# Three and a half score tiles for images two to four, with column sums and small operations moved to other steps

## The chip, the cores and the metric

The kernel runs on one core of a Trainium2 chip. Its metric is the device time of one execution in microseconds (us); the figure to beat is the median of the runs shown. A core has a matrix engine (TensorE, PE in the rows; PEld is its loading of weights), a vector engine (VectorE, DVE), a scalar engine (ScalarE, ACT), GpSimd (POOL), and SyncE (SP), which here only issues transfers. Matrix products land in PSUM, which has eight banks for each of 128 partitions; everything else works in SBUF.

## What is computed

An attention over 4 images of 448 rows with 12 heads of 64, in which the heads are mixed before and after the softmax, and on its result (1,792 rows of 768) an RMS norm and a gated network:

```python
scores = scale * np.matmul(q, k.transpose(0, 1, 3, 2))
scores = np.einsum('bhij,hg->bgij', scores, w_pre)
scores = scores - np.max(scores, axis=-1, keepdims=True)
attn = np.exp(scores)
attn = attn / (np.sum(attn, axis=-1, keepdims=True) + 1e-09)
attn = np.einsum('bhij,hg->bgij', attn, w_post)
y = np.matmul(attn, v)                      # x: (4*448, 768), heads side by side
rms = np.sqrt(np.mean(x * x, axis=-1, keepdims=True) + 1e-06)
xn = x / rms * rms_g
g = xn @ w_gate
silu = g * (1.0 / (1.0 + np.exp(-g)))
out = silu * (xn @ w_val) @ w_out
```

## The kernel before

**Chunks and steps.** Each image's 448 rows are cut into four chunks (`n` counts them, 0 to 15, four to an image) of 120, 120, 110 and 98 rows. A chunk is worked off in 6, 6, 6 and 5 *steps* `(n, p)`. This gives 92 steps, numbered 0 to 91 here. The first steps of the chunks are 0, 6, 12, 18 | 23, 29, 35, 41 | 46, 52, 58, 64 | 69, 75, 81, 87. The attention runs from 0 to about 345 us; then comes the gated network.

**What stands in a step.** `part_a` emits every engine's work by hand, step by step, and each engine takes its own in that order. In step t, which works on `(n, p)`:
- PE makes the *premix* `sp`, the scores of 20 query rows mixed over the heads. It is four products of 64x64 weights `wk_pre` with `r`, two for each half of the rows of PE, into two PSUM banks.
- DVE takes the two row maxima `nm` (`rowmax`). ACT makes the two exponentials `e` (`expo`) and sums each as it goes. `norm` adds 1e-9 (`t`, DVE), takes the reciprocal (`rp`, DVE) and scales the weights of the second mix with it (`wn`, two operations on GpSimd).
- PE makes the *postmix* `pm` of the step before, which needs that step's `e` and `wn`. ACT and DVE copy a half each into `at_all` (`evac_a`).
- PE makes one or two pieces of `av`, attention times `v`, for an earlier pair of chunks (`av_at`). ACT copies finished ones into `xt` (`av_copy`).
- PE makes one *score unit* `qk` of a later chunk (`qk_at`): the products of `q` and `k` for a pair of heads, again four products into two banks. Its second half stands between the two halves of the premix, its first behind them. ACT copies one bank out into `st`, DVE the other (`qk_evac`). Transfers on SP's queue then regroup the rows of `st` into `r`, in which heads and rows lie as the premix wants them. `r` has three tiles, one for every third chunk.

**Units and their order.** A chunk has six score units, one a step, in a plain list: five ahead of step 0, then one for each of the steps 0 to 84. Steps 85 to 91 have none. A fourth chunk has only 98 rows but takes six units as well.

**Work on the side.** GpSimd squares and adds up finished rows (`sum_ops`: L318, L325, L332, L333), one operation a step up to step 80 and two from then on, emitted ahead of `norm`'s `wn`. When an image is complete, PE makes its column sums `pss` (`column_sums`, L347, into a bank of the score units); a chain of small operations turns them into the reciprocal root (`rsqrt`; DVE first, then GpSimd), and `x_scale_ops` follows. PE makes `pss` at the end of the steps 40, 63 and 84. From step 23 on DVE also converts the weights of the gated network, an operation of about 0.35 us a step (`first_w`, tile `wac`), and other small chains. `lows` are low halves of a split, emitted by `flush`. Loads of `q`, `k` and `v` are jobs with a fixed step (`job`).

Of the kernel before, what the change touches and what calls it, by code (L numbers as in the profile page):

```python
# [7 lines left out]
F32 = mybir.dt.float32  # L8
# [16 lines left out]
GROUPS = [12, 12, 12, 9]  # L25
# [26 lines left out]
def attention_moe(ctx: ExitStack, tc, q, k, v, wpre, wpost, mask, ident, wgv, wo, rms_g, out):  # L52
# [33 lines left out]
    wk_pre = cst.tile([128, 64], F32, name="wk_pre")  # L86
    wk = cst.tile([128, HR], F32, name="wk")

    msk = pro.tile([128, 2, RH], F32, name="msk", tag="ksm1")
    we = pro.tile([128, H], F32, name="we", tag="ksm2")  # L90
    wp = pro.tile([128, H], F32, name="wp", tag="ksm3")

    def load_consts():
        nc.sync.dma_start(msk.rearrange("p a r -> p (a r)"), mask)
        nc.sync.dma_start(we, wpre)
        nc.sync.dma_start(wp, wpost)

# [28 lines left out]
    held = []  # L126
# [7 lines left out]
    def qk_mm(n, hp):  # L134
# [6 lines left out]

        return [[lambda j=j, u=u: one(j, u) for u in range(2)] for j in range(2)]
# [8 lines left out]

    def qk_evac(n, hp, j):
        h, np_ = 2 * hp + j, PAIRS[n % NC]
        ps = qps[n, hp][j]
        if n == 0 and h < 1 or n == 1 and h < 2 * AHEAD:
            st = pro.tile([128, S], F32, name="st", tag="st", bufs=11)
        else:
            st = pq.tile([128, S], F32, name="st", tag="st", bufs=12)
        if j:
            nc.vector.tensor_copy(st, ps[:, :S])  # L160
        else:
            nc.scalar.activation(st, ps[:, :S], AF.Copy)
        for i, (lo, hi) in enumerate(((0, EARLY), (EARLY, 2 * np_)) if n == 0 else ((0, GROUPS[n % NC]),)):
            w, at_ = RH * (hi - lo), 2 * RH * lo
            if h < H - 1:
                parts = [(h, 2 * RH, at_, 2 * w)]
            else:
                parts = [(h, RH, at_, w), (64, RH, at_ + w, w)]
            for row, k_, src, many in parts:
                dst = rt[n][row : row + (k_ - 1) * GAP + 1 : GAP, lo:hi]  # L170
                if i:
                    held.append((dst, st[src : src + many]))
                else:
# [1086 lines left out]
```

## Time and profile before

| | us |
|---|---|
| median of 3 runs | 827.72 |
| lowest, highest | 825.3, 830.05 |
| profiled execution, own time | 822.48 |
| its span | 820.6 |
| PE busy | 794.4 |
| DVE busy | 634.5 |
| ACT busy | 507.3 |
| GpSimd busy | 350.4 |

The span goes from the first to the last recorded instruction; the execution's own time is a little longer. An engine's busy time counts the time in which at least one of its instructions runs. PE is near its limit on the average, but the average covers the gated network, where it hardly pauses, and the attention, where several engines take turns.

### The profile page before, as it was taken

What the parts mean: (1) busy time and instruction counts of PE and PEld (TensorE: products, weight loads), DVE (VectorE), ACT (ScalarE), POOL (GpSimd) and SP (SyncE); (2) the same over time, 40 slices, a digit from 0 to 9 for tenths busy, and PEclk for the clock granted to TensorE, in tenths of its full rate; (3) what the DMA queues carried; (4) which work ended last, traced back from release to release, by engine and by line L of the source; (5) the groups of instructions that cost most, each with busy time, mean ns of one, the idle gap of its engine ahead of it and who ended that gap; (6) DMA issues with size and microseconds to landing.
All of it is one profiled execution on the core that took longest, in us unless ns stands there. A gap on an engine that the chain in (4) does not pass through costs nothing.

```text
span 820.6 us, 26914 instructions
## 1 busy us (share of the span) xinstructions
PE 794.4 (97%) x10806; PEld 485.2 (59%) x10806; DVE 634.5 (77%) x1322; ACT 507.3 (62%) x1133; POOL 350.4 (43%) x467
## 2 busy tenths in 40 slices
PE   7899999999999989899999999999999999999998
PEld 2567777767776767655555555555555555555555
DVE  5777878888798867888788978997889676547562
ACT  3677778777776867664344454545444546969850
POOL 7212343454355435843624433426144359452310
PEclk9999999999999999999999999999999999999999
DMA  7777777777876754564255644754546446566641
GB/s 216 208 216 217 219 229 222 228 219 232 222 234 200 211 147 150 158 230 118 66 177 150 183 129 127 216 149 121 174 145 201 133 127 184 157 199 176 184 135 67
DMA packets 81902, 145.15 MB, mean 177 GB/s; under 512 B 10527, under 2 KB 72797, under 8 KB 81779
## 3 DMA queue, kind: packets, MB, share of 16 engines
q1 hardware_dynamic: 79982, 139.83, 57.0%
q0 software_dynamic: 832, 2.06, 1.0%
q8 instruction: 85, 1.39, 0.7%
q10 hardware_dynamic: 965, 1.56, 0.6%
q14 instruction: 38, 0.31, 0.1%
HBM read 72.83 MB, written 31.88 MB: 128 GB/s over the span
## 4 chain that ended last, share of the span: by engine, by line
PE 86%; DMA 8%; DVE 2%; issue 1%; ACT 1%; POOL 1%; SPq 0%; ACTq 0%; DVEq 0%; POOLq 0%
PE qk L140 7%; PE pm L226 7%; PE sp L187 7%; PE av L294 6%; PE pg L750 6%; PE pg L752 6%; PE pv L752 6%; PE pg L751 6%; PE pv L751 6%; PE pv L750 6%; DMA r<-st 6%; PE po L751 6%; PE po L750 6%; PE po L752 6%; DMA wraw<-in_wgv 1%
## 5 line engine op out<-in xcount | busy, mean ns | idle before, releaser
L187 PE MATMUL sp<-r,wk_pre 64*64 64x448 f32 x720 | 167.4, 542 | 5.4 <-DMA r<-st 3.5
L203 ACT ACTIVATE e<-sp,nm 128x448 f32<-128x448 f32 x180 | 114.3, 637 | 84.8 <-DVE nm L196 82.4
L140 PE MATMUL qk<-k,q 64*64 64x448 f32 x768 | 152.6, 559 | 5.9 <-DMA q<-in_q 4.1
L196 DVE TENSOR_REDUCE nm<-sp 128x1 f32<-128x448 f32 x180 | 110.3, 620 | 44.1 <-PE sp L187 27.4
L215 POOL TENSOR_SCALAR wn<-wk,rp 128x60 f32<-128x60 f32 x180 | 59.5, 345 | 181.8 <-DVE rp L212 109.7
L226 PEld LDWEIGHTS pm<-wn,e 60*64 60x64 f32 x5040 | 106.1, 134 | 37.6 <-POOL wn L215 23.8
L226 PE MATMUL pm<-wn,e 60*64 60x60 f32 x5040 | 106.7, 220 | 4.2 <-issue 4.1
L798 POOL TENSOR_TENSOR sg<-sg,u 128x448 f32<-128x448 f32 x36 | 45.9, 1275 | 151.2 <-ACT sg L795 106.7
L294 PE MATMUL av<-at_all,v 64*64 64x240 f32 (+6 forms) x1728 | 93.6, 316 | 4.6 <-issue 2.6
L750 PE MATMUL pv<-x,wh 128*128 128x448 f16 x264 | 93.0, 352 | 0.0
L752 PE MATMUL pv<-x,wl 128*128 128x448 f16 x264 | 93.0, 352 | 0.0
L752 PE MATMUL pg<-x,wl 128*128 128x448 f16 x264 | 93.0, 352 | 0.0
L751 PE MATMUL pv<-x,wh 128*128 128x448 f16 x264 | 93.0, 352 | 0.0
L751 PE MATMUL pg<-x,wh 128*128 128x448 f16 x264 | 93.0, 352 | 0.0
L750 PE MATMUL pg<-x,wh 128*128 128x448 f16 x264 | 93.0, 352 | 0.0
L750 PE MATMUL po<-h,fac 128*128 128x448 f16 (+1 forms) x258 | 89.8, 348 | 0.0
L751 PE MATMUL po<-h,fac 128*128 128x448 f16 (+1 forms) x258 | 89.8, 348 | 0.0
L752 PE MATMUL po<-h,fac 128*128 128x448 f16 (+1 forms) x258 | 89.8, 348 | 0.0
L750 PEld LDWEIGHTS <-wh 128*128 128x128 f16 x528 | 51.7, 98 | 48.2 <-issue 0.2
L751 PEld LDWEIGHTS <-wh 128*128 128x128 f16 x528 | 51.7, 98 | 48.3 <-issue 0.3
L752 PEld LDWEIGHTS <-wl 128*128 128x128 f16 x528 | 51.7, 98 | 48.2
L187 PEld LDWEIGHTS sp<-r,wk_pre 64*64 64x64 f32 x720 | 60.3, 133 | 27.2 <-ACT e L203 13.2
(167 smaller groups left out, 1567.3 us busy)
## 6 DMA issues: line engine op xcount, KB each, us to landing
r<-st SPq DMA_DIRECT2D x117, 210.0 KB
hraw<-td SPq DMA_DIRECT2D x84, 224.0 KB
wraw<-in_wgv SPq DMA_DIRECT2D x20, 768.0 KB
td<-keep SPq DMA_DIRECT2D x48, 224.0 KB
wraw<-in_wo SPq DMA_DIRECT2D x12, 768.0 KB
r<-st SPq DMA_DIRECT2D x44, 157.5 KB
v<-in_v SPq DMA_DIRECT2D x24, 256.0 KB
k<-in_k SPq DMA_DIRECT2D x24, 224.0 KB
```

What stands on the lines that cost most here:

```text
L140: nc.tensor.matmul(ps[j][m, :S], qt[n][sl, hp, m], kt[n // NC, hp][sl], start=True, stop=True)
L187: nc.tensor.matmul(o, wk_pre[sl], rt[n][sl, 2 * p + v_], start=True, stop=True)
L196: nc.vector.tensor_reduce(t, ps[:, :S], AX.X, ALU.max, negate=True)
L203: nc.scalar.activation(e, ps[:, :S], AF.Exp, bias=nmx.pop((n, p, u)), accum_out=sm[n, p][:, u : u + 1])
L215: nc.gpsimd.tensor_scalar(wn[n, p][:, u], wk, r[:, u : u + 1], 1.0, ALU.mult, ALU.mult)
L226: nc.tensor.matmul(o[:, :, at_], e_[sl, j : j + JT], w_[sl].rearrange("p (s i) -> p s i", s=2), start=True, stop=True)
L294: nc.tensor.matmul(x, vt[b, hp][sl, j, c_], a, start=(c_ == 0), stop=(c_ == JC - 1))
L750: nc.tensor.matmul(ps, a, xh[:, kk, at_], start=(kk == 0), stop=False)
L751: nc.tensor.matmul(ps, a, xl_[:, kk, at_], start=False, stop=False)
L752: nc.tensor.matmul(ps, a2, xh[:, kk, at_], start=False, stop=(kk == KT - 1))
L798: nc.gpsimd.tensor_tensor(h, sg, u, ALU.mult)
```

## The change

- **Shared score units.** In images two to four (chunks from 4 on) the chunks 0 to 2 of an image fill all 128 rows of a score tile: 8 more rows belong to the fourth chunk. What remains of the fourth chunk are 50 rows, which fit half a tile (64). A unit of such a *shared* chunk (`shared(n)`; n = 7, 11, 15) therefore makes four heads at once (`two`) instead of two, each bank holding two heads, and both row halves of PE write into one bank, bank by bank. Such a chunk takes three units instead of six.
- **`rest`.** The extra rows don't go into `r` but into a tile of their own, `rest`, to every second row of it (`rest_out`). The first and the last premix of a shared chunk read `rest` with a second variant of the weights `wk_pre`. GpSimd clears `rest` in the steps 3 and 7.
- **Order of the units.** A unit of chunk n stands no earlier than one step after the first of chunk n - 2. Together with the fewer units this leaves the steps 34, 35, 57, 58 and 80 to 91 without score products.
- **Column sums.** `pss` moves from the steps 40, 63 and 84 to 57, 79 and 84. Its chain keeps its bits in SBUF rather than in the PSUM bank, with three operations on DVE rather than four; `x_scale_ops` go one a step.
- **`t`** is made by GpSimd for all chunks but the last.
- Of the `lows` one is emitted behind the row maxima and up to two later in the step; loads of `q` and `k` get steps to suit; `st` becomes one tile with a place for each head; `first_w_ops(0)` starts six steps later.

```diff
+def shared(n):
+    return n >= NC and n % NC == NC - 1
...
-    wk_pre = cst.tile([128, 64], F32, name="wk_pre")
+    wk_pre = cst.tile([128, 2, 64], F32, name="wk_pre")
+    rest = cst.tile([128, 4, S], F32, name="rest")
...
         b, c = divmod(n, NC)
+        wide = 64 if shared(n) else 128
         if not hp:
-            qt[n] = pq.tile([128, H // 2, 128], F32, name=f"q{n}", tag="q", bufs=2)
-        hp = slice(hp, hp + many)
-        eng.dma_start(qt[n][:, hp], q[b, :, c, hp])
+            qt[n] = pq.tile([128, H // 2, wide], F32, name=f"q{n}", tag="q", bufs=2)
+        src = q[b, :, c * H // 2 * 128 + hp * wide : c * H // 2 * 128 + (hp + many) * wide]
+        eng.dma_start(qt[n][:, hp : hp + many].rearrange("p h w -> p (h w)"), src)
...
-    held = []
+    held, waiting = [], []
+    st_all = pq.tile([128, H, S], F32, name="st", tag="st")
...
+        def two(j, i):
+            sl, u = slice(64 * j, 64 * j + 64), (i + j) % 2
+            nc.tensor.matmul(ps[i][64 * u : 64 * u + 64, :S], qt[n][sl, 2 * hp + i], kt[n // NC, 2 * hp + i][sl], start=True, stop=True)
+
+        if shared(n):
+            return [[lambda j=j, i=i: two(j, i) for j in (i, 1 - i)] for i in range(2)]
         return [[lambda j=j, u=u: one(j, u) for u in range(2)] for j in range(2)]
...
+    def rest_out(n, half, st):
+        if shared(n):
+            for i in range(2):
+                for u in range(2):
+                    rows = slice(100 + 12 * u, 112 + 12 * u)
+                    nc.sync.dma_start(rest[rows, slot(n - 3 + i)], st[64 * u + 60 + 2 * i : 64 * u + 62 + 2 * i, :6])
+        else:
+            nc.sync.dma_start(rest[4 + half : 4 + half + 95 : 2, slot(n)], st[120:, 6 * half : 6 * half + 6])
...
+        last = shared(n)
+        kind = int(last and p in (0, PAIRS[-1] - 1))
...
+        def rows(sl, i):
+            if not kind:
+                return rt[n][sl, i - 2 * last]
+            return rest[sl, slot(n - 3 + (i if p == 0 else 2))]
 
...
             sl = slice(64 * u, 64 * u + 64)
-            nc.tensor.matmul(o, wk_pre[sl], rt[n][sl, 2 * p + v_], start=True, stop=True)
+            nc.tensor.matmul(o, wk_pre[sl, kind], rows(sl, 2 * p + v_), start=True, stop=True)
...
-        nc.vector.tensor_scalar(t, s, 1e-9, None, ALU.add)
+        (nc.gpsimd if n < NCHUNK - 1 else nc.vector).tensor_scalar(t, s, 1e-9, None, ALU.add)
...
-            sq[b, "ops"] = rsqrt(ps[:JP, :JC], b, const, nc.gpsimd, ps[:JP, JC : 2 * JC])
+            sq[b, "ops"] = rsqrt(ps[:JP, :JC], b, const, nc.gpsimd)
...
-        ops = [lambda o=o: nc.vector.tensor_scalar(o, v, 1.0 / DM, 1e-6, ALU.mult, ALU.add) for o in {id(x): x for x in (bits, var)}.values()]
-        ops += [
-            lambda: nc.vector.tensor_scalar(i, bits.bitcast(I32), 1, None, ALU.logical_shift_right),
+        ops = [
+            lambda: nc.vector.tensor_scalar(var, v, 1.0 / DM, 1e-6, ALU.mult, ALU.add),
+            lambda: nc.vector.tensor_scalar(i, var.bitcast(I32), 1, None, ALU.logical_shift_right),
...
-    for i, a in enumerate([(n, hp) for n in range(1, NCHUNK) for hp in range(H // 2)][AHEAD:]):
-        qk_at[i].append(a)
+    starts, t_ = {}, -1
+    for n in range(1, NCHUNK):
+        for hp in range(H // 4 if shared(n) else H // 2):
+            if n == 1 and hp < AHEAD:
+                continue
+            t_ = max(t_ + 1, first[n - 2] + 1 if n > 1 else 0)
+            starts.setdefault(n, t_)
+            qk_at[t_].append((n, hp))
...
-                job(6 * n - 16 + 3 * i, load_q, n, 3 * i, 3, nc.sync)
+                job(starts[n] - 5 + (1 if shared(n) else 3) * i, load_q, n, 3 * i, 3, nc.sync)
...
-    chain(first[4] + 29, lambda: first_w_ops(0), 2)
+    chain(first[4] + 35, lambda: first_w_ops(0), 2)
     chain(first[4] + 56, lambda: first_w_ops(1), 3)
...
-        t = first[NC * b + NC + 2] + (5 if b < B - 2 else 3)
-        for i in range(17):
-            last_at[t + max(i - 2, 0) // 3].append((sq_all, b, i))
-        chain(t, lambda b=b: x_scale_ops(b), 2 if b < B - 2 else 4)
+        t = (first[10] - 1, first[13] + 4, first[14] + 3)[b]
+        for i in range(16):
+            last_at[t + (max(i - 1, 0) if i < 4 else 3 + (i - 4) // 3)].append((sq_all, b, i))
+        chain((first[6] + 8, first[10] + 6, first[14] + 3)[b], lambda b=b: x_scale_ops(b), 1 if b < B - 2 else 4)
...
                 rowmax(*back(0))
-                flush()
+                flush(1)
                 expo(*back(0))
...
+            flush()
...
+            if t in (3, 7):
+                nc.gpsimd.memset(rest[:, t // 2 - 1 : t // 2 + 1], 0.0)
...
-    nc = bacc.Bacc("TRN2", target_bir_lowering=False, num_devices=1)
+    nc = bacc.Bacc("TRN2", target_bir_lowering=False, num_devices=1, dynamic_dma_scratch_size=8192)
```

On PE, from step 31 of the kernel before; `q_2195` are the queries of chunk 7, `r_123` and `r_121` the tiles of chunks 5 and 6, the rows from a first `sp` to the next `pm` are a step's premix and score unit (rows of the steps 32 and 33, which read likewise with `k_1` and `k_2`, stand between the first and the second piece):

```order
L187 MATMUL sp<-r_123,wk_pre 64x448 x2
L140 MATMUL qk<-k_0_827,q_2195 64x448 x2
L187 MATMUL sp<-r_123,wk_pre 64x448 x2
L140 MATMUL qk<-k_0_827,q_2195 64x448 x2
L226 MATMUL pm<-wn,e 64x2x30 x28
```

```order
L187 MATMUL sp<-r_123,wk_pre 64x448 x2
L140 MATMUL qk<-k_3_1036,q_2195 64x448 x2
L187 MATMUL sp<-r_123,wk_pre 64x448 x2
L140 MATMUL qk<-k_3_1036,q_2195 64x448 x2
L226 MATMUL pm<-wn,e 64x2x30 x28
L294 MATMUL av<-at_all,v_2_1337 64x220 x8
L187 MATMUL sp<-r_121,wk_pre 64x448 x2
L140 MATMUL qk<-k_4_1104,q_2195 64x448 x2
```

The second piece is step 34 and the start of 35, each with a unit of chunk 7. On PE in the changed kernel, from step 33 (`q_2131` are the queries of chunk 7, `r_126` and `r_124` the tiles of chunks 5 and 6):

```order
L232 MATMUL sp<-r_126,wk_pre 64x448 x2
L153 MATMUL qk<-k_5_1133,q_2131 64x448 x2
L232 MATMUL sp<-r_126,wk_pre 64x448 x2
L153 MATMUL qk<-k_4_1064,q_2131 64x448 x2
L271 MATMUL pm<-wn,e 64x2x30 x28
L339 MATMUL av<-at_all,v_1_1131 64x220 x4
L339 MATMUL av<-at_all,v_1_1131 64x2x55 x4
L232 MATMUL sp<-r_126,wk_pre 64x448 x4
L271 MATMUL pm<-wn,e 64x2x30 x28
L339 MATMUL av<-at_all,v_2_1291 64x220 x8
L232 MATMUL sp<-r_124,wk_pre 64x448 x4
```

Step 33 has the last unit of chunk 7, of four heads (two tiles of `k`); 34 and 35 go from the premix to the postmix with no unit between. Around the column sums, on PE before, the end of step 40 and the start of 41 (`k_4_3002`, `q_2672`: a unit of chunk 8; `sum_1495`: the sums of the first image):

```order
L294 MATMUL av<-at_all,v_5_2512 64x240 x4
L294 MATMUL av<-at_all,v_5_2512 64x2x60 x4
L347 MATMUL pss<-ones,sum_1495 112x1 x4
L187 MATMUL sp<-r_122,wk_pre 64x448 x2
L140 MATMUL qk<-k_4_3002,q_2672 64x448 x2
L187 MATMUL sp<-r_122,wk_pre 64x448 x2
```

and in the changed kernel, step 57 and the start of 58 (`sum_1446`: the same sums):

```order
L232 MATMUL sp<-r_124,wk_pre 64x448 x4
L271 MATMUL pm<-wn,e 64x2x30 x28
L339 MATMUL av<-at_all,v_2_2913 64x220 x8
L392 MATMUL pss<-ones,sum_1446 112x1 x4
L232 MATMUL sp<-r_125,wk_pre 64x448 x4
L271 MATMUL pm<-wn,e 64x2x30 x28
```

Before, a premix with a score unit stands behind `pss`; now a premix and a postmix. On DVE an ordinary step before reads

```order
L196 TENSOR_REDUCE nm<-sp 128x1 x2
L160 COPY st<-qk 128x448
L263 COPY at_all<-pm 128x2x42x5
L210 TENSOR_SCALAR t<-s 128x2
L212 RECIPROCAL rp<-t 128x2
L564 TENSOR_SCALAR wac<-wraw 128x384
```

and in the changed kernel

```order
L241 TENSOR_REDUCE nm<-sp 128x1 x2
L194 COPY st<-qk 128x448
L308 COPY at_all<-pm 128x2x42x5
L257 RECIPROCAL rp<-t 128x2
L613 TENSOR_SCALAR wac<-wraw 128x384
```

with `t` gone from between the copy and `rp`. On GpSimd two steps with additions of sums read so in the changed kernel (L363 is L318 of before, L370 is L325):

```order
L363 TENSOR_TENSOR xt_1692<-xt_1692,xt_1693 128x480
L255 TENSOR_SCALAR t<-s 128x2
L260 TENSOR_SCALAR wn<-wk,rp 128x60 x2
L370 TENSOR_TENSOR xt_1693<-xt_1692 128x480
L255 TENSOR_SCALAR t<-s 128x1
```

Here `t` stands behind the addition of its step and ahead of `wn`; before, `wn` alone stood there.

## Rows read from the trace of the kernel before

**Rows 1.** The page: the head.

```profile
span 820.6 us, 26914 instructions
```

**Rows 2.** Busy time by stretch: us, PE, PEld, DVE, ACT, POOL, PEclk, DMA, GB/s.

```profile
61.90:294.60 232.70, 222.75 (x5956) 172.97 (x5952) 192.13 (x517) 173.78 (x474) 100.88 (x220) 1.00 0.76 220
345.00:820.60 475.60, 472.40 (x2624) 247.24 (x2622) 360.70 (x618) 263.20 (x484) 194.32 (x145) 1.00 0.51 156
```

**Rows 3.** DVE's timeline, steps 30 and 31: start, us, what, [idle before <-releaser].

```profile
120.83 0.62 DVE L196 TENSOR_REDUCE nm<-sp 128x1 f32<-128x448 f32 x1
...
122.79 0.59 DVE L263 COPY at_all<-pm 128x420 f32<-128x420 f32 x1
123.29 0.16 DVE L210 TENSOR_SCALAR t<-s 128x2 f32<-128x2 f32 x1
123.55 0.17 DVE L212 RECIPROCAL rp<-t 128x2 f32<-128x2 f32 x1
...
126.98 0.62 DVE L196 TENSOR_REDUCE nm<-sp 128x1 f32<-128x448 f32 x1
```

**Rows 4.** DVE's timeline, a step without `av`.

```profile
49.75 0.60 DVE L196 TENSOR_REDUCE nm<-sp 128x1 f32<-128x448 f32 x1
50.89 0.62 DVE L196 TENSOR_REDUCE nm<-sp 128x1 f32<-128x448 f32 x1 [0.54 <-PE sp L187]
...
52.80 0.60 DVE L196 TENSOR_REDUCE nm<-sp 128x1 f32<-128x448 f32 x1
```

**Rows 5.** PE's timeline, a step with two pieces of `av`.

```profile
319.90 1.64 PE L294 MATMUL av<-at_all,v 64*64 64x240 f32 x31
```

**Rows 6.** PE's timeline, end of step 40 and start of 41.

```profile
156.27 0.95 PE L347 MATMUL pss<-ones,sum 128*112 128x1 f32 x8
157.15 1.00 PE L187 MATMUL sp<-r,wk_pre 64*64 64x448 f32 x8
157.95 1.19 PE L140 MATMUL qk<-k,q 64*64 64x448 f32 x8
```

**Rows 7.** DVE's timeline, step 85 and the first maxima of 86.

```profile
312.96 1.13 DVE L196 TENSOR_REDUCE nm<-sp 128x1 f32<-128x448 f32 x2
...
315.23 0.17 DVE L212 RECIPROCAL rp<-t 128x2 f32<-128x2 f32 x1
...
316.08 1.10 DVE L196 TENSOR_REDUCE nm<-sp 128x1 f32<-128x448 f32 x2
```

**Rows 8.** DVE's timeline, the first maxima of steps 82 and 84.

```profile
299.22 0.62 DVE L196 TENSOR_REDUCE nm<-sp 128x1 f32<-128x448 f32 x1 [0.73 <-PE qk L140]
...
307.06 0.63 DVE L196 TENSOR_REDUCE nm<-sp 128x1 f32<-128x448 f32 x1 [0.96 <-PE qk L140]
```

**Rows 9.** DVE's timeline, the first maxima of steps 40 and 41.

```profile
154.03 0.62 DVE L196 TENSOR_REDUCE nm<-sp 128x1 f32<-128x448 f32 x1
...
159.22 1.15 DVE L196 TENSOR_REDUCE nm<-sp 128x1 f32<-128x448 f32 x2
```

**Rows 10.** Waits of PE and PEld, 61.9 to 313 us: total, times, longest.

```profile
PE sp L187 <- DMA r<-st: 1.5, 4, 0.6
PEld sp L187 <- DMA r<-st: 1.1, 1, 1.1
```

**Rows 11.** ACT's timeline, the end of the second sum in step 30.

```profile
122.97 0.19 ACT L203 ACTIVATION_READ_ACCUMULATOR e<-sp,nm 128x1 f32 x1
```

**Rows 12.** GpSimd's line L372: ns shortest/median/longest, first and last start.

```profile
L372 POOL TENSOR_TENSOR u<-y x9: 198/200/203, 162.4 to 325.2; 112x4 f32<-112x4 f32 x9
```

**Rows 13.** GpSimd's timeline, step 30.

```profile
123.89 0.60 POOL L215 TENSOR_SCALAR wn<-wk,rp 128x60 f32<-128x60 f32 x2 [1.61 <-DVE rp L212]
```

**Rows 14.** GpSimd's groups of instructions: count | busy us, mean ns | idle before.

```profile
L318 POOL TENSOR_TENSOR xt<-xt,xt 128x480 f32<-128x480 f32 (+3 forms) x27 | 29.9, 1106 | 0.0
```

**Rows 15.** PE's timeline, the premix of step 91.

```profile
334.00 0.96 PE L187 MATMUL sp<-r,wk_pre 64*64 64x448 f32 x1
...
334.12 0.96 PE L187 MATMUL sp<-r,wk_pre 64*64 64x448 f32 x1
```

More of the change, by code (lines that the diff above doesn't have):

```diff
@@ L150, in alone, with gather @@
         in_turn(*parts)
+    def gather(n, h, src, lo, hi, held_):
+        w, at_ = RH * (hi - lo), 2 * RH * lo
+        if h < H - 1:
+            parts = [(h, 2 * RH, at_, 2 * w)]
+        else:
+            parts = [(h, RH, at_, w), (64, RH, at_ + w, w)]
+        for row, k_, from_, many in parts:
+            dst = rt[n][row : row + (k_ - 1) * GAP + 1 : GAP, lo:hi]
+            x = src[from_ : from_ + many]
+            if held_:
+                held.append((dst, x))
+            else:
+                turn = h if row < H else h + 1
+                if n:
+                    eng = nc.gpsimd if n == 1 and 6 <= h < 2 * AHEAD else nc.sync
+                else:
+                    eng = nc.sync if turn % 2 else nc.gpsimd if turn < 6 else nc.scalar
+                eng.dma_start(dst, x)
@@ L163, in qk_evac @@
[L163 to L173, printed above, removed]
[L174 to L179 removed]
+        at_ = 2 * hp + j
@@ new lines, in qk_evac @@
+        st = st_1 if n == 1 else st_all
+        if j:
+            nc.vector.tensor_copy(st[:, at_], qps[n, hp][j][:, :S])
+        else:
+            nc.scalar.activation(st[:, at_], qps[n, hp][j][:, :S], AF.Copy)
+        if j and n >= NC and hp % 3 == 2:
+            rest_out(n, hp // 3, st)
+        if shared(n):
+            for u in range(2):
+                waiting.append((n, 2 * (2 * hp + j) + (u + j) % 2, st[64 * u : 64 * u + 64, at_], 0, SPLIT, False))
+            if at_ < 3 or at_ == 5:
+                for args in waiting:
+                    gather(*args)
+                waiting.clear()
+        else:
+            for i, (lo, hi) in enumerate(((0, EARLY), (EARLY, H)) if n == 0 else ((0, H if n % NC < NC - 1 else WHOLE),)):
+                gather(n, at_, st[:, at_], lo, hi, i)
@@ L181, in premix @@
+    def rest_out(n, half, st):
+        if shared(n):
+            for i in range(2):
+                for u in range(2):
+                    rows = slice(100 + 12 * u, 112 + 12 * u)
+                    nc.sync.dma_start(rest[rows, slot(n - 3 + i)], st[64 * u + 60 + 2 * i : 64 * u + 62 + 2 * i, :6])
+        else:
+            nc.sync.dma_start(rest[4 + half : 4 + half + 95 : 2, slot(n)], st[120:, 6 * half : 6 * half + 6])
     def premix(n, p):
@@ L439, in attention_moe @@
             if n % NC == NC - 1 and n + 1 < NCHUNK:
-                job(t + 1, load_k, n // NC + 1, hp)
+                for i in (2 * hp, 2 * hp + 1) if shared(n) else (hp,):
+                    job(t + 1, load_k, n // NC + 1, i)
     chains = []
@@ L1223, in layout @@
     eye_r = np.eye(RH, dtype=np.float32)
-    mix = np.zeros((2, 64, H), np.float32)
-    row = np.zeros((2, 64, RH), np.float32)
+    mix = np.zeros((128, 2, H), np.float32)
+    row = np.zeros((128, 2, RH), np.float32)
     for u in range(2):
         for r in range(RH):
-            at = GAP * r + (np.arange(H) + u) % H
-            mix[u, at], row[u, at] = inputs["w_pre"], eye_r[r]
+            for h in range(H):
+                hp, j = divmod(h, 2)
+                half, i = divmod(h, H // 2)
+                unit, odd = divmod(hp, 2)
+                if not u or r < 3:
+                    at = 4 + half + 2 * (6 * (RH * u + r) + i)
+                else:
+                    at = 100 + 12 * ((j + odd) % 2) + 6 * (r - 3) + 2 * unit + odd
+                for kind, x in enumerate((64 * u + GAP * r + (h + u) % H, at)):
+                    mix[x, kind], row[x, kind] = inputs["w_pre"][h], eye_r[r]
     return {
```

97 lines of the change are left out of this document (48 added, 49 removed).

## Prediction

> **What bounds the kernel now.** I read the profile in this order: busy time by stretch, then the vector engine's (DVE) timeline of single steps, then TensorE's (PE) timeline and waits. The execution behind the rows spans 820.6 us [rows 1]; its own time was 822.48 us. The runs shown have a median of 827.72 us, 5.24 us more, so I make the sum against 822.48 us and carry the difference over to the median.
>
> The expert network after 345 us keeps PE busy 472.40 of 475.60 us [rows 2]. The change touches nothing there, so whatever is gained or lost must lie in the attention steps.
>
> A step starts where DVE takes the first row maximum `nm`. Two ordinary steps, each with one pair of score products and one piece of `av`, run from 120.83 to 126.98 us: 3.08 us per step [rows 3]. A step without any `av` runs from 49.75 to 52.80 us, 3.05 us [rows 4], although PE has some 0.8 us less to do (two pieces are 1.64 us [rows 5]). So PE alone does not set the length: the second `nm` waits 0.54 us for premixed scores [rows 4], which stand behind a score product that waits until DVE has copied the last one out (`st`). An ordinary step is thus a balance of PE's amount and the loop `nm`, `e`, `t`, `rp`, next `nm`. A score pair is as large as a premix, and from the start of a premix to that of the score pair behind it PE takes 0.80 us (157.15 to 157.95 [rows 6]). Taking 0.80 us off PE does not take 0.80 us off the step.
>
> Steps without score products exist already, 85 to 91. One runs from 312.96 to 316.08 us, 3.12 us, with two pieces of `av` [rows 7]. In it DVE gets from the first `nm` (312.96) to the end of `rp` (315.40) in 2.44 us [rows 7]; that is what the loop needs when there is no score copy to make.
>
> **The change part by part.**
>
> *Nine steps lose their score products.* Images two to four need 21 units where they needed 24, so 76 of 92 steps carry one instead of 85. By the order of the program the freed steps are 34, 35, 57, 58, 80, 81 (one piece of `av` each) and 82, 83, 84 (two pieces each).
> - With two pieces, steps 82 and 83 took 7.84 us (299.22 to 307.06), 3.92 each [rows 8]. The same without score products takes 3.12 [rows 7]. The difference is PE's 0.80 of a score pair, in full. Three steps by 0.80 are 2.4 us. Bounds: 1.5 us if the GpSimd queue (below) spoils part of it, 2.7 us.
> - With one piece, PE would need 3.12 less 0.8, or 2.3 us, so the loop binds. Its 2.44 us is the lower bound for a step, 3.08 the upper. I take 2.78, nearer to the loop, because the second premix still waits for the second `e` and steps 34 and 58 keep a weight conversion on DVE behind `rp`. Six by 0.30 are 1.8 us; bounds 0 and 6 by 0.64, 3.8.
>
> *The column sums `pss` move.* Now they stand in steps 40, 63 and 84. Step 40 ran from 154.03 to 159.22, 5.19 us, 2.1 over an ordinary one [rows 9]. On PE they are 0.95 us, and afterwards the next premix (157.15) and its score pair (157.95) come behind them [rows 6]. The new places are 57, 79 and 84. The 0.95 us on PE stay, and so does the premix after them, but no score pair and no copy follow, and DVE has two small operations fewer. I take 0.4 us of gain for each, 1.25 us in all; bounds 0 and 3.
>
> *Transfers of `r` come earlier before their use.* PE waited 1.5 us in four places for `r` between 61.9 and 313 us, and its weight loads 1.1 us more [rows 10]. In the changed order the last score unit of chunk 8 is emitted 5 steps ahead of its use (4 before), that of chunks 12 to 14 5 steps (3 before), of 15 8 (3 before). I take 2.0 us, bounds 0.5 and 2.6. SP issues 26 more transfers, but they carry the same rows: a fourth chunk had 12 by 90 = 1,080 rows of 1,792 bytes, now 12 by 60, 3 by 96 and 48, which is 1,056. DMA engines were 0.76 busy [rows 2], so I cost this at nothing; if that cover were gone it would show as waits for `r`, and the 2.0 us would be lost.
>
> *`t` goes from DVE to GpSimd in 87 steps.* On DVE it starts at 123.29 and `rp` at 123.55, 0.26 later [rows 3]. But the accumulation that it needs had ended at 123.16 [rows 11]: `t` stood behind the copy `at_all` (122.79) [rows 3]. On GpSimd it can start at 123.16 plus a handover. No row shows `t` there. The nearest are a small GpSimd operation, 0.20 us [rows 12], and the handover from `rp` (ends 123.72 [rows 3]) to `wn` (123.89), 0.17 us [rows 13]. Then `t` ends at 123.16 + 0.17 + 0.20 = 123.53, and `rp` starts at 123.70 instead of 123.55. By these rows it costs 0.15 us in a step where `rp` holds up the next `nm`; by the quicker handover within DVE, 0.10 from the end of `t` to `rp`, it costs nothing. `nm` waits for premix anyway in most steps, so I take 0.5 us for all 87, bounds a gain of 1 and, if it counted everywhere, a loss of 13.
> On GpSimd `t` also queues behind the column-sum additions of its step, 1.1 us each in the mean [rows 14]. One of them fits before `t` is due. From step 81 two stand there, about 2 us, and 0.6 us of `wn` ahead of them. I take 0.7 us for steps 83 to 86, bounds 0 and 2.
>
> *The rest*: clearing `rest` in two steps, a wider `wk_pre`, splitting the low halves from step 87 on over two places, conversions of scales one at a time. Each is hidden under a step that something else ends, and I cost them together at nothing, with 1 us either way.
>
> *A half chunk's two heads in one bank.* Unit `two` writes one PSUM bank from both row halves of PE, which a score pair never did. In step 91 the premix does so: the two row halves start at 334.00 and 334.12 and each takes 0.96 us [rows 15]; they overlap, so I add nothing. The Trainium skill, TensorEngine Tiling (Array Packing), section Gotcha 1: PSUM Pressure, says that different row tiles cannot use the same PSUM bank at the same time. By that rule the nine units would be made in passes and the gain would be gone (rival 4); by the row nothing is added.
>
> **Sum.** 2.4 + 1.8 + 1.25 + 2.0 - 0.5 - 0.7 = 6.25 us. 822.48 less 6.25 is 816.2 us, and on the scale of the median 827.72 less 6.25 is 821.5 us, 0.75% faster.
>
> **The rivals.**
> 1. *PE's amount counts in full.* If the single-piece steps drop to the loop's 2.44 (3.8 us) and `pss` loses its whole excess (3), the sum is 2.7 + 3.8 + 3.0 + 2.6 - 1.2 = 10.9, hence 816.8 us. For it: the loop alone can do 2.44 [rows 7]. Against: the premix still waits for `e`, and `pss` keeps its 0.95 us.
> 2. *The gain is caught by the next limit.* Single-piece steps stay at 3.05 as the step without `av` does [rows 4], `pss` costs the same in its new place, and instruction stalls eat the shorter waits: 2.4 + 0.5 less 1.2 leaves 1.7, hence 826.0 us.
> 3. *Slower: GpSimd's `t` lengthens the loop.* Each of the 87 steps with `t` there has `rp`, and behind it the next `nm`, later by up to 0.15 us. At 0.12 us a step it costs 10.4 us against 6.95 + 0.5 of gain: about +3, hence 831 us. It decides from 0.09 us a step on. For it: in DVE's queue the next `nm` stands behind `rp`. Against: in the step of [rows 4] the second `nm`, which ends the loop, has 0.54 us to spare after the first.
> 4. *One bank serves one row half at a time.* The four products of a shared unit then take three passes of 0.80 us instead of one, 1.6 us more a unit, 14.4 us for nine, of which I let half be hidden under the postmix: 7.2 less the forecast's 6.25 is +0.95, hence 828.7 us. The overlap in [rows 15] speaks against it; the page named above speaks for it.
>
> **How the numbers follow.** Forecast 0.52, rival 1 0.15, rival 2 0.19, rival 3 0.10, rival 4 0.04. The runs shown differ by 4.75 us among themselves, so about 0.5%, 4.1 us, is what a measurement of this kernel can tell from no change. Of the forecast (own range 818.5 to 824.5) four fifths lie beyond 0.5%; with rival 1 that makes 0.56 faster. Slower by over 0.5% are two fifths of rival 3 and a little of rival 4, 0.06. The rest is 0.38. For 8 in 10 the range takes in rivals 1 and 2 with half of the scatter of a median beyond each: 814.8 to 827.8.
>
> **What would show it.** Right: steps 82 and 83 at 3.1 us and steps 80 and 81 below 3; no wait of PE for `r` after step 45; step 40 ordinary and step 57 near 4; `rp` starting no later after the second `e` than now. Wrong: DVE's `rp` waiting for GpSimd's `t` by several tenths in ordinary steps; steps 31 to 33, 54 to 56 and 77 to 79 (shared units) longer than their neighbours; single-piece steps without score products still at 3.05 us.

## The result, and the profile after

The changed kernel takes 831.99 us (median of 20 runs, 826.66 to 838.77), the kernel before 827.17 us (20 runs beside it): a ratio of 1.0065, interval 1.0043 to 1.0087. The change costs 0.65%, some 5.4 us (4.8 by the two medians), where the prediction had it gain 6.25. The ratios here and below leave out runs more than 1.5% above the fastest of their kernel, among them one of 4,612.52 us beside this result and five of the twelve of experiment 3. The profiled execution of the changed kernel took 832.17 us, right at its median; the one of before, 822.48 us, lies 4.7 us under the median that twenty runs gave. So the two spans, 9.8 us apart, show about twice the price, and below no difference of two profiles is taken for a price.

The page's head, and busy time by stretch (us, PE, PEld, DVE, ACT, POOL, PEclk, DMA, GB/s), of the changed kernel:

```profile
span 830.4 us, 26817 instructions
```

```profile
354.80:830.40 475.60, 470.85 (x2558) 245.76 (x2556) 359.92 (x616) 262.60 (x481) 193.44 (x144) 1.00 0.51 155
61.90:300.00 238.10, 221.19 (x5795) 168.00 (x5795) 178.22 (x428) 170.52 (x462) 110.66 (x269) 1.00 0.73 213
```

The last 475.60 us, the network, keep PE as busy as before [rows 2], and from the network's first product `pg` to the end it is 491.7 us, against 492.0 before. The loss lies in the attention, as the prediction had it. Now the steps. DVE's timeline, first maxima of steps 80 to 84 with the wait of `rp` between, which answers to [rows 8]:

```profile
303.30 1.16 DVE L241 TENSOR_REDUCE nm<-sp 128x1 f32<-128x448 f32 x2 [1.08 <-PE sp L232]
...
305.72 0.17 DVE L257 RECIPROCAL rp<-t 128x2 f32<-128x2 f32 x1 [0.76 <-POOL t L255]
...
306.38 1.14 DVE L241 TENSOR_REDUCE nm<-sp 128x1 f32<-128x448 f32 x2
...
309.39 1.14 DVE L241 TENSOR_REDUCE nm<-sp 128x1 f32<-128x448 f32 x2
...
312.85 0.62 DVE L241 TENSOR_REDUCE nm<-sp 128x1 f32<-128x448 f32 x1 [0.39 <-PE sp L232]
...
315.88 1.15 DVE L241 TENSOR_REDUCE nm<-sp 128x1 f32<-128x448 f32 x2
```

Steps 80 and 81 take 3.08 and 3.01 us, 82 takes 3.46 and 83 takes 3.03. All four are shorter than in the profile before (4.98, 4.58, 3.80 and 4.03). DVE's timeline around the old and the new place of the first image's column sums, which answers to [rows 9]:

```profile
158.37 1.38 DVE L241 TENSOR_REDUCE nm<-sp 128x1 f32<-128x448 f32 x2
...
161.45 0.61 DVE L241 TENSOR_REDUCE nm<-sp 128x1 f32<-128x448 f32 x1
...
218.27 1.15 DVE L241 TENSOR_REDUCE nm<-sp 128x1 f32<-128x448 f32 x2 [0.22 <-ACT at_all L310]
...
222.81 0.16 DVE L421 TENSOR_SCALAR var<-pss 112x4 f32<-112x4 f32 x1 [1.97 <-PE pss L392]
...
223.79 0.62 DVE L241 TENSOR_REDUCE nm<-sp 128x1 f32<-128x448 f32 x1 [0.55 <-PE sp L232]
```

Step 40 is ordinary now (3.08 us instead of 5.19), step 57 takes 5.52. What is new shows in the waits (total us, times, longest). DVE's and PE's from 61.9 to 330 us:

```profile
DVE rp L257 <- POOL t L255: 10.9, 27, 1.3
DVE at_all L308 <- PE pm L271: 9.8, 9, 2.0
DVE st L194 <- DMA rest<-st: 8.2, 4, 3.0
```

```profile
PE pm L271 <- issue: 8.5, 6, 2.2
PE qk L149 <- DVE st L194: 2.1, 2, 1.4
PE qk L149 <- issue: 2.0, 2, 1.4
PE sp L232 <- issue: 1.9, 1, 1.9
```

PE no longer waits for `r` [rows 10]. Instead DVE's copy `st` waits 8.2 us in four places for a transfer to `rest`, a wait that the prediction does not name. The longest of the four, step 59, on DVE and on SP's queue:

```profile
228.33 0.62 DVE L241 TENSOR_REDUCE nm<-sp 128x1 f32<-128x448 f32 x1 [0.57 <-PE sp L232]
231.93 0.62 DVE L194 COPY st<-qk 128x448 f32<-128x448 f32 x1 [2.98 <-DMA rest<-st]
```

```profile
224.48 1.04 SPq L116 DMA_DIRECT2D k<-in_k  x2
225.73 2.77 SPq L215 DMA_DIRECT2D rest<-st  x4
228.54 5.68 SPq L184 DMA_DIRECT2D r<-st  x7
```

Chunk 11 is a shared one; its third unit is that of step 56, which ended at 218.27. That unit's four transfers to `rest` are issued 7.5 us later and its seven to `r` from 10.3 us later on. Step 59 has the first unit of chunk 12, which copies into the places of `st` that those four transfers read. It took 6.52 us, against 4.07 before.

The lag of SP's queue can be read for every transfer to `r`: from the end of the last copy `st` that it carries to the start of its issue, matched in the order of the program for the chunks from 2 on. Its mean is 2.7 us in the trace before and 5.9 in that of the changed kernel (*lag* below).

Part of this is SP's own time. The issues of the 30 transfers to `rest` (ns shortest/median/longest, first and last start; 18 of 48 rows each, 12 of 12 rows each):

```profile
L217 SPq DMA_DIRECT2D rest<-st x18: 727/737/776, 79.4 to 292.1; - x18
L215 SPq DMA_DIRECT2D rest<-st x12: 612/633/708, 141.0 to 303.6; - x12
```

That is some 21 us of SP. Between the first maxima of steps 23 and 85 SP is issuing for 73% of the time in the trace before (158.1 of 215.7 us) and for 83% in that of the changed kernel (184.7 of 223.5 us), while the DMA engines' mean busy share goes from 0.76 to 0.73 in the rows shown for the two kernels.

### The profile page after: what moved, and what is told of

Read it like the earlier page. It is cut to its first block, busy times and chain, and to the rows that moved or that the text cites. A ratio compares the mean times of both kernels' runs of the same rounds, so it can differ in the third digit from the quotient of the medians.

```text
span 830.4 us, 26817 instructions
## 1 busy us (share of the span) xinstructions
PE 796.7 (96%) x10734; PEld 479.8 (58%) x10734; DVE 618.8 (75%) x1224; ACT 504.5 (61%) x1124; POOL 371.2 (45%) x556
## 4 chain that ended last, share of the span: by engine, by line
PE 87%; DMA 4%; issue 3%; DVE 2%; ACT 2%; POOL 1%; ACTq 0%; SPq 0%; DVEq 0%; POOLq 0%
PE pm L271 8%; PE sp L232 8%; PE qk L149 8%; PE av L339 6%; PE pg L800 6%; PE pg L801 6%; PE pv L802 6%; PE pv L801 6%; PE pg L802 6%; PE pv L800 6%; PE po L801 6%; PE po L800 6%; PE po L802 6%; DMA rest<-st 2%; DMA xr<-xd 1%
## 5 line engine op out<-in xcount | busy, mean ns | idle before, releaser
L232 PE MATMUL sp<-r,wk_pre 64*64 64x448 f32 x684 | 153.1, 542 | 5.0 <-ACT e L248 3.0
L149 PE MATMUL qk<-k,q 64*64 64x448 f32 x624 | 119.2, 566 | 11.3 <-DMA q<-in_q 4.0
L339 PE MATMUL av<-at_all,v 64*64 64x240 f32 (+6 forms) x1728 | 91.1, 314 | 1.1 <-issue 1.1
L339 PEld LDWEIGHTS av<-at_all,v 64*64 64x64 f32 x1728 | 69.4, 133 | 5.6 <-issue 2.8
```

Of the source, the lines that this page charges most:

```text
L149: nc.tensor.matmul(ps[j][m, :S], qt[n][sl, hp, m], kt[n // NC, hp][sl], start=True, stop=True)
L232: nc.tensor.matmul(o, wk_pre[sl, kind], rows(sl, 2 * p + v_), start=True, stop=True)
L339: nc.tensor.matmul(x, vt[b, hp][sl, j, c_], a, start=(c_ == 0), stop=(c_ == JC - 1))
```

## The experiments

Ratios are to the kernel before on the same chip, with a 95% interval; the result and the experiments were not all on one chip. Times in us that come from ratios are shares of 827 us. Theory A: the copies `st` wait for the new transfers, because they stand late on SP's queue. Theory B: `t` on GpSimd lengthens the steps. Theory C: PE's stalls with nothing to wait for ("issue", 13.5 us against 7.0 in the profiles).

**1. Without the 30 transfers to `rest`.** The scores of the extra rows are left out; `rest` stays zero.

```diff
-        if j and n >= NC and hp % 3 == 2:
-            rest_out(n, hp // 3, st)
```

> The changed kernel without the 30 transfers from st to rest; the extra rows' scores are left out (rest stays zero). Theory A (the score copies st wait for these transfers, 8.2 us in four steps, since they stand late in SP's queue): 8 to 10 us less than the changed kernel, about 0.995 to 0.997 of the kernel before, and no wait of st for a transfer. Theory B (t on GpSimd lengthens the steps without scores): at most 2 us less, about 1.004. Theory C (PE's instruction stalls, 13.5 us against 7.0 before): stalls stay, about 1.005.

0.9941 (0.9905 to 0.9976), 822.74 us against 825.46 beside it. The waits of `st` for `rest` are gone, the lag is 3.3 us, and step 59 takes 3.76 us. DVE's timeline there:

```profile
219.94 1.38 DVE L239 TENSOR_REDUCE nm<-sp 128x1 f32<-128x448 f32 x2 [0.27 <-PE qk L149]
221.23 0.61 DVE L194 COPY st<-qk 128x448 f32<-128x448 f32 x1
...
223.70 0.62 DVE L239 TENSOR_REDUCE nm<-sp 128x1 f32<-128x448 f32 x1 [0.47 <-PE qk L149]
```

The transfers cost 1.0065 less 0.9941, 1.24% or 10 us, with both intervals 7 to 14; by the differences of the medians it is 7.5 us. Without them the rest of the change gains 4.9 us.

**2. The 30 transfers issued by ScalarE.**

```diff
-                    nc.sync.dma_start(rest[rows, slot(n - 3 + i)], ...)
+                    nc.scalar.dma_start(rest[rows, slot(n - 3 + i)], ...)
...
-            nc.sync.dma_start(rest[4 + half : 4 + half + 95 : 2, slot(n)], ...)
+            nc.scalar.dma_start(rest[4 + half : 4 + half + 95 : 2, slot(n)], ...)
```

> The same 30 transfers, but issued by ScalarE rather than on SP's queue. Theory A with the queue as its cause: they are issued within 1 us of the copy rather than 2 to 8.5 us later, the waits of st vanish, 4 to 8 us less than the changed kernel, 0.997 to 1.002 of before; SP also gets 21 us of issuing less. If instead the transfers themselves are slow or contend, the waits of st stay and the time is 1.0065 or worse. Theories B and C: 1.005 to 1.007.

1.0746 (1.0694 to 1.0798). A miss: SP's own queue now waits for them.

```profile
SPq L184 <- DMA rest<-st: 61.4, 16, 8.5
```

In the trace each transfer signals its landing on one of eight semaphores, used in turn by SP and ScalarE (77 or 78 transfers on each), and most (541 of 622 here) stand behind a wait for that semaphore's last transfer. That ScalarE takes its transfers late, in its own order of work, and SP stands behind them is the reading of the row above; ScalarE also spends 0.68 us on each of the longer ones, and the two costs were not separated.

**3. `t` back on DVE.**

```diff
-        (nc.gpsimd if n < NCHUNK - 1 else nc.vector).tensor_scalar(t, s, 1e-9, None, ALU.add)
+        nc.vector.tensor_scalar(t, s, 1e-9, None, ALU.add)
```

> Only t goes back to DVE. Theory B: DVE waited 10.9 us for t in 27 places, 0.5 to 1.3 us each in steps 80 to 86; with t on DVE steps 80 to 83 fall below 3 us, 4 to 6 us less, about 1.000 of before. Theory A and C: under 2 us less, 1.004 to 1.0065.

1.0015 (0.9976 to 1.0053), as Theory B has it; by the medians (828.61 and 825.46 us) it is 1.0038, about where A and C had it. And steps 80 and 81 hardly get shorter: DVE's first maxima of 80, 81 and 82 stand 3.03 and 2.96 us apart, against 3.08 and 3.01.

```profile
292.41 1.16 DVE L241 TENSOR_REDUCE nm<-sp 128x1 f32<-128x448 f32 x2 [0.71 <-PE sp L232]
295.44 1.14 DVE L241 TENSOR_REDUCE nm<-sp 128x1 f32<-128x448 f32 x2
298.40 1.14 DVE L241 TENSOR_REDUCE nm<-sp 128x1 f32<-128x448 f32 x2
```

**4. Other instructions ahead of step 0.**

```diff
-        for _ in range(4):
-            nc.tensor.matmul(busy[:, :S], ones, kt[0, 0], start=True, stop=True)
+        for _ in range(20):
+            nc.tensor.matmul(busy[:, :80], ones, kt[0, 0][:, :80], start=True, stop=True)
```

> The changed kernel with the four wide warm-up products before step 0 replaced by twenty narrow ones: 16 products more for PE, some 64 more instructions, nothing else. Theory C, in the form that a stall comes where the reload of PE's instructions meets a burst of short products: the stalls move to other steps and their sum changes by 3 us or more either way (1.002 to 1.011). If the stalls come from the traffic of the transfers, they stay in steps 27, 28, 50, 51, 57, 59 and 73, and the time stays within 0.2% of 1.0065.

1.0072 (1.0036 to 1.0108). The stalls did move and shrank to 3.8 us of PE's waits, and the time stayed. Steps 36 and 59 took 8.48 and 8.63 us instead; in 36 PE waited for a load of `k` on SP's queue.

```profile
PE pm L271 <- issue: 2.6, 6, 0.9
...
PE qk L149 <- DMA k<-in_k: 2.1, 1, 2.1
PE av L339 <- issue: 1.2, 3, 0.6
```

So the sum of the stalls in one profile (Theory C) does not follow the time. That other waits took their place is not excluded: steps 36 and 59 are 3.8 and 2.1 us longer than in the changed kernel's trace.

**5. The places of `st` in turn.** The first unit after a shared chunk writes places that the chunk before last used.

```diff
+    def place(n, h):
+        return (h + 6 * (max(n // NC - 1, 0) % 2)) % H
+
     def qk_evac(n, hp, j):
-        at_ = 2 * hp + j
+        h = 2 * hp + j
+        at_ = place(n, h)
...
```

> The changed kernel, but the halves of the twelve places of st are taken in turn, so that the first units after a shared chunk (steps 36 and 59) write places used six steps before and not three to five, which the last of the four small transfers still read. If these places are the trouble (A1): no wait of st for a transfer in 36 and 59, 3 to 5 us less than the changed kernel, 1.000 to 1.003 of before. If SP's queue is the trouble, with 13 transfers of r, four of rest and six loads of k in three steps (A2): the delay shows elsewhere, as waits for k or r, and under 1.5 us are won, 1.005 to 1.0065.

1.0041 (1.0008 to 1.0073). The waits of `st` fall from 8.2 to 2.0 us, and steps 36 and 59 take 4.1 and 3.8 us, but only about 2 us are won, less than expected by A1 (the places are the trouble) and within the two intervals.

```profile
DVE st L198 <- DMA rest<-st: 2.0, 2, 1.1
```

**6. The same with `t` on DVE** (edits 5 and 3 together).

> The kernel of the run before with t on DVE as well. If the two costs are independent, their gains add: 0.996 to 0.9985 by A1, about 1.000 by A2.

1.0067 (1.0032 to 1.0102): the two gains do not add. `st` waits 1.9 us, but now PE's score unit in step 39 waits 3.07 us, and the step takes 8.80 us. The trace puts the wait down to a transfer on SP's queue, `xd`; this is a store that a score unit does not read, so which transfer it was stays open.

```profile
PE qk L149 <- DMA xd<-xt: 3.1, 1, 3.1
```

**7. The kernel before with `t` on GpSimd** (edit 3 the other way round).

> The kernel before with t on GpSimd for all chunks but the last, nothing else. If t costs in every step (0.06 us and more): 1.005 to 1.010. If it costs only where no scores leave room, which here are steps 85 and 86 and those with two additions of sums: 1.000 to 1.002.

0.9999 (0.9965 to 1.0033). DVE's `rp` waits as often for `t` as in the changed kernel, and it costs nothing that can be told from zero (the interval is 2.9 us of gain to 2.7 of loss):

```profile
DVE rp L212 <- POOL t L210: 8.7, 26, 0.8
```

**8. Shared units in every second step,** with the edits 5 and 3.

```diff
-            t_ = max(t_ + 1, first[n - 2] + 1 if n > 1 else 0)
+            t_ = max(t_ + (2 if shared(n) and hp else 1), first[n - 2] + 1 if n > 1 else 0)
```

> As the second of these (places in turn, t on DVE), and the three units of a shared chunk stand in every second step (31, 33, 35; 54, 56, 58; 77, 79, 81) instead of three in a row, with the same number of steps without scores. If the burst on SP's queue is the trouble (A2): steps 36 and 59 fall to 3 to 4 us with no wait for k, r or rest, and 3 to 6 us less than the run with places and t: 0.990 to 0.996 of before. If places alone were (A1): the same as that run.

1.0050 (1.0020 to 1.0080), no gain over the run before last. The lag stays at 6.1 us, and the wait moves on once more: in step 40 PE waits for `k`, and step 59 takes 9.57 us, with a wait of 2.62 us of PE's score unit for nothing that the trace shows.

```profile
156.63 1.00 PE L149 MATMUL qk<-k,q 64*64 64x448 f32 x8 [2.28 <-DMA k<-in_k]
```

The next four ask what it is in the 30 transfers that costs. Theory Q: their number, on SP's queue. Theory B is from here on: what they carry.

**9. Each transfer to `rest` cut to one row.** In both branches the 12 or 48 rows become one (`rows = slice(100 + 12 * u, 101 + 12 * u)`; `rest[4 + half : 5 + half, slot(n)]`).

> The changed kernel with all 30 transfers to rest, each cut to one row of 1,792 bytes (of 12 or 48; the extra rows' scores are left out). From the end of a copy st to the issue of its transfer to r it took 2.7 us in the mean before, 5.9 in the changed kernel and 3.3 in the run without the 30 transfers. Theory Q (their number fills SP's queue, whatever they carry): the lag stays at 5 to 6 us and the time at 1.003 to 1.008 of before. Theory B (what they carry, 48 rows from 8 partitions, is slow and holds st): lag about 3.3 us, 0.992 to 0.997.

0.9994 (0.9960 to 1.0028), lag 4.7 us: between the two theories. An issue to `rest` still holds SP for 0.57 to 0.59 us (medians of the two kinds). By the middle values the number makes 4.4 us of the 10 and the contents 5.9, but the intervals are as wide as that. As in run 1, scores of the extra rows are left out.

**10. Loads of `q` and `k` issued by ScalarE.**

```diff
-        (nc.sync if b else nc.sync).dma_start(t, k[b, :, hp])
+        (nc.scalar if b else nc.sync).dma_start(t, k[b, :, hp])
...
-                job(starts[n] - 5 + (1 if shared(n) else 3) * i, load_q, n, 3 * i, 3, nc.sync)
+                job(starts[n] - 5 + (1 if shared(n) else 3) * i, load_q, n, 3 * i, 3, nc.scalar)
```

> The changed kernel, whole, with the loads of q (from chunk 3 on) and of k (from image two on), some 39 issues, moved from SP's queue to ScalarE. Theory Q: the lag falls below 3.5 us, the waits of st shrink, 5 to 9 us less than the changed kernel, 0.995 to 1.000 of before, unless the 0.4 to 0.6 us of each issue stand on ScalarE's way to e. Theory B: no gain, 1.005 or more.

1.0466 (1.0409 to 1.0524), and

**11. the same in the kernel before.**

> The same move of loads in the kernel before, as a control. Theory Q: SP's queue has room there, the lag falls from 2.7 to about 2 us and the time by under 3 us, 0.996 to 1.001. If ScalarE's issues cost by themselves: above 1.002.

1.0730 (1.0685 to 1.0775). 44 issues move (613 on SP become 569, and 583 become 539), not 39 as the expectations have it. In both SP waits for transfers of ScalarE, as in run 2; this is SP's queue in the kernel before with this edit:

```profile
SPq L179 <- DMA q<-in_q: 66.5, 13, 7.3
SPq L179 <- DMA k<-in_k: 18.3, 6, 5.7
```

The Trainium skill, DMA: Bandwidth & Descriptors, section Issuing engines are not separate DMA queues, says that starting transfers on several engines only saves the sequencer's time for it. The trace agrees that no speed is to be had that way. Here the time was 4.7 and 7.3% worse, while SP waits 85 us in the two rows above.

**12. The kernel before with 30 transfers of 64 bytes more.**

```diff
+        if j and n >= NC and hp % 3 == 2:
+            for i in range(2 if n % NC == NC - 1 else 1):
+                nc.sync.dma_start(more[i : i + 1], st[120:121, :16])
...
```

> The kernel before with 30 transfers of 64 bytes from st added on SP's queue, in the steps of the same units (two for a chunk, four for a fourth chunk), into a tile that nobody reads. Theory Q: the lag rises to 4 us or more and the time to 1.003 to 1.010. Theory B: 0.999 to 1.002.

1.0037 (1.0003 to 1.0071), lag 3.6 us: some 3 us for 30 transfers that carry next to nothing. This speaks for number, barely beyond the interval, and with less lag than Theory Q had expected (4 us).

**13 to 16. Fewer, larger loads.** `q` of a chunk in one transfer, `k` in pairs: by the traces 22 transfers less on SP's queue (591 instead of 613; 561 instead of 583 in the kernel before), not the 34 of the expectations, in the changed kernel (13), with the places in turn (14), in the kernel before (15), and with places and `t` on DVE (16).

```diff
...
-            for i in range(2):
-                job(starts[n] - 5 + (1 if shared(n) else 3) * i, load_q, n, 3 * i, 3, nc.sync)
+            job(starts[n] - 5, load_q, n, 0, 6, nc.sync)
...
-                for i in (2 * hp, 2 * hp + 1) if shared(n) else (hp,):
-                    job(t + 1, load_k, n // NC + 1, i)
+                if shared(n) or hp % 2:
+                    job(t + 1, load_k, n // NC + 1, 2 * hp if shared(n) else hp - 1, 2)
```

> The changed kernel, whole, with its loads in fewer transfers of the same bytes: q of a chunk in one instead of two, k of images two to four in pairs. SP's queue has 373 rows instead of 407 (381 before). Theory Q (the number of transfers on SP's queue): the lag from a copy st to the issue of its transfer falls from 5.9 to about 3.5 us and the time by 3 to 7 us, to 0.998 to 1.003 of before. If only what rest carries counts (its 48 rows hold st): no change, 1.005 to 1.008.

> The same with the halves of st taken in turn. By theory Q with the wait of st as a second part: another 1 to 4 us, 0.993 to 1.000; by Q alone as the run before.

> The kernel before with the same fewer loads, 347 rows on SP's queue instead of 381. The lag is 2.7 us there; theory Q: it falls to about 2 us, the time by 0 to 3 us, 0.996 to 1.000.

> As the second of these, with t on DVE. If t on GpSimd costs 2 us or more once the queue is relieved: 0.990 to 0.997; if it costs nothing: within 0.2% of the second.

1.0078 (1.0043 to 1.0113), 1.0058 (1.0026 to 1.0091), 1.0081 (1.0038 to 1.0124) and 1.0026 (0.9987 to 1.0064). What Theory Q forecast was missed each time; 13 lies where the other branch had it (1.005 to 1.008). In 13 the lag fell to 4.1 us as Theory Q wants, and the time did not follow; in 14 the waits of `st` are gone as well, and it did not follow either:

```profile
DVE st L204 <- DMA rest<-st: 0.4, 1, 0.4
```

The control (15) has a lag of 2.1 us and is slower than the kernel before by 0.8%. So neither the number on SP's queue nor the lag sets the time by itself. That larger loads hold up the small transfers behind them would fit, and was not tested.

**17 and 18. The nine freed steps alone.** In the kernel before, the last three units of chunks 7, 11 and 15 are left out with their copies; in 17 their 21 transfers to `r` too, in 18 these are issued all the same.

```diff
...
+    def dropped(n, hp):
+        return n >= NC and n % NC == NC - 1 and hp >= 3
+
     def qk_evac(n, hp, j):
         h, np_ = 2 * hp + j, PAIRS[n % NC]
+        if dropped(n, hp):
+            gather(n, h, keep[n, h - 6]) if SEND else None
+            return
...
+        keep[n, h] = st
...
-            if qk_at[t]:
+            if qk_at[t] and not dropped(*qk_at[t][0]):
                 qk = qk_mm(*qk_at[t][0])
```

> The kernel before without the last three score units of chunks 7, 11 and 15, their copies and their 21 transfers to r (those scores are left out, r keeps older rows): nine steps (34 to 36, 58 to 60, 82 to 84) lose their score products and nothing else changes, no rest, t on DVE, column sums where they were. By the prediction's sum this is worth 4.2 us, with bounds of 1.5 and 6.5: 0.992 to 0.998 of before. If the freed steps are worth nothing because other limits catch them: 0.999 to 1.001.

> The same, but the 21 transfers to r are issued all the same, from the copies of three units earlier. If the gain is PE's, as the prediction has it: the same time as the run before within 0.2%. If the gain is that of the transfers: back to 0.998 to 1.001.

0.9980 (0.9948 to 1.0012) and 0.9961 (0.9930 to 0.9992), a gain of 1.7 and 3.2 us by the middle values, with 1.0 of loss to 4.3 of gain and 0.7 to 5.8 of gain by the intervals. The gain does not hang on the transfers: the run that sends them is, if anything, the faster. In 18 a freed step with one piece of `av`, 58, takes 2.70 us:

```profile
216.95 1.15 DVE L209 TENSOR_REDUCE nm<-sp 128x1 f32<-128x448 f32 x2
219.65 1.15 DVE L209 TENSOR_REDUCE nm<-sp 128x1 f32<-128x448 f32 x2
```

## Why the prediction was wrong

It was wrong in sign: a gain of 6.25 us was forecast and 5.4 were lost. The step that failed is "SP issues 26 more transfers, but they carry the same rows [...], so I cost this at nothing". The runs put 10 us in its place (1 against the changed kernel); the transfers are also 30 more, not 26 (613 on SP, 583 before). The prediction counted bytes and looked for a loss at PE's waits for `r`. It missed two things. The 30 transfers stand on a queue that works in order, and each takes 0.63 to 0.74 us of SP's time; behind the third unit of a shared chunk four of them stand together with seven of the chunk's thirteen to `r`, beside the next image's `k`. And they read `st`, so that a later copy has to wait until they have landed. Neither needed the changed kernel's trace: the queue's rows and the distance between a place's two uses are in the order of the program.

Without the transfers the rest of the change gains 4.9 us (2.0 to 7.9 by the interval), not far from the sum's 6.25, but this does not show the terms one by one. The other steps, by the terms of the sum:

- **Nine freed steps: 4.2 us (bounds 1.5 and 6.5).** Measured by themselves 1.7 and 3.2 us (17, 18). By the middle values the size was too large by 1 to 2.5 us, but both intervals take in 4.2. A single-piece step can fall below the 2.78 us assumed (35 takes 2.61 in the changed kernel, 58 takes 2.70 in 18), but 80 and 81 stayed near 3.0 in the changed kernel, with `t` on either engine (3).
- **`pss`: 1.25 us.** Between the two profiles the steps 40 and 63 get shorter by 2.11 and 1.35 us, 57 and 79 longer by 0.81 and 1.02, and 84 by 0.17, which leaves a gain of 1.5 us. But 57 and 84 are also freed steps, so part of this belongs to the term above; these are single profiles, and in 57 PE stalls with nothing to wait for in both. The size is not shown more closely than that. That step 57 would be near 4 us was wrong (5.52).
- **Waits for `r`: 2.0 us.** PE's are gone, its weight loads have one of 0.6 us left. But the place that waits has moved to `st`, in runs 4 and 8 to `k`, and in 6 to a transfer that the trace does not tell. The condition given, "if that cover were gone it would show as waits for `r`", named the wrong waiter.
- **`t`: -0.5 and -0.7 us, rival 3.** Four pairs of runs differ only in it: 1.0065 and 1.0015, 1.0041 and 1.0067, 1.0058 and 1.0026, 0.9999 and 1. The mean is 0.14% or 1.1 us for GpSimd, with a scatter of twice that: nothing that can be told from zero. Rival 3, 0.12 us in every step, is excluded by 7 (10 us would be 1.012). The 8 to 11 us that `rp` waits for `t` cost nothing that 7 can tell from zero; that something else would have ended most of these waits as late is a reading of it. In an ordinary step the handovers were quicker than the nearest rows had made them. The sum on ACT ends at 126.52, and on GpSimd and DVE:

```profile
126.32 0.20 ACT L248 ACTIVATION_READ_ACCUMULATOR e<-sp,nm 128x1 f32 x1
```

```profile
126.61 0.21 POOL L255 TENSOR_SCALAR t<-s 128x2 f32<-128x2 f32 x1 [1.10 <-ACT e L248]
```

```profile
126.86 0.17 DVE L257 RECIPROCAL rp<-t 128x2 f32<-128x2 f32 x1
```

  From the sum's end to `rp` it is 0.34 us, where [rows 11] and [rows 3] give 0.39 before and the prediction allowed 0.54.
- **Two heads in one bank, rival 4.** PE's timeline of the changed kernel, start and end of a pair's unit beside a premix and then of a shared unit beside one:

```profile
204.66 0.59 PE L149 MATMUL qk<-k,q 64*64 64x448 f32 x2
...
205.71 0.54 PE L149 MATMUL qk<-k,q 64*64 64x448 f32 x2
```

```profile
207.74 0.56 PE L153 MATMUL qk<-k,q 64*64 64x448 f32 x1
...
208.92 0.78 PE L153 MATMUL qk<-k,q 64*64 64x448 f32 x2
```

  From the first start to the last end the pair's unit takes 1.60 us and the shared one 1.96. Over the trace the nine shared units take 1.72 to 1.97 us, 1.92 in the median, and the pairs' units 1.64. So "I add nothing" was too little by 0.28 us a unit on PE, 2.5 us for the nine at most; of the 1.6 us a unit of rival 4 there is no trace. The Trainium skill, TensorEngine Tiling (Array Packing), section Gotcha 1: PSUM Pressure, lets no two row tiles use one bank at the same time. The trace shows no passes of 0.80 us one after another; whether the 0.28 us come from the bank or from the other order of the products was not tested. The steps hardly show it: 31 to 33 take 9.5 us in the changed kernel's profile and 9.3 before, 54 to 56 take 9.4 and 9.5.

**What stays open.** How the transfers cost 10 us. In one profile `st` waits 8.2 us for them; where that wait was mostly taken away (5, 14) the time fell by 2 us at most, while elsewhere others waited: PE for `k` in 4 and 8, for a transfer not told in 6, and for nothing that the trace shows in step 36 of 14 (8.63 us) and step 59 of 8 (9.57 us). That the queue's tail is late and whoever stands there waits is what these traces show. Number and contents share it (9, 12), in parts that these intervals don't tell apart, and fewer but larger transfers are no remedy (13 to 16). Run 15 is slower by 0.8% with less lag and fewer transfers, so regrouping the loads alone cost the kernel before as much as the whole change did; how much of the 10 us is of that kind was not tested. The traces of 3, 5, 8, 13 and 14 are each of the shortest of the executions measured, so they may show fewer waits than the median has. No version that computes the whole beat the kernel before.

## What to carry to other kernels

A new transfer on a queue that works in order is costed by its place there: what stands behind it, how long its issue holds the issuing engine, how late the queue runs already, and what may not be overwritten until it has landed. Bytes and busy shares of the DMA engines did not show this here; the share of time in which SP issues (73%) and the lag from a producer's end to the issue of its transfer could be read from the trace before the change. When one late wait is taken away and the time stays, look for the next waiter on the same queue before looking for another cause. And a profile is one execution: the two here lie 9.8 us apart where the medians lie 4.8 apart.

## What the runs showed of the hardware that was not expected

- Transfers issued by ScalarE can hold up those of SP: the completion semaphores are shared in turn, and moving 30 or 44 issues cost 4.7 to 7.5%.
- The small transfers here take about as long whatever they carry: from issue to its last completion event the median in the changed kernel's trace was 5.8 us for the 205 of SP to `r`, 5.6 for loads of `q` and 5.2 for those to `rest`, and with one row each, in run 9, still 4.7 (5.2 for those to `r` there).
- Issuing holds SP for much the same time too: 0.63 and 0.74 us (medians) for 12 and 48 rows to `rest`, 0.59 and 0.57 for one row.
- Two row halves of PE that write into one bank of PSUM cost little more than with a bank each: 1.92 us for a unit in the median, against 1.64.
